# Phi one tile later and in one VectorE operation, small loads, one activation table and a reordered second phase, in a linear-attention and routed-MLP kernel

## The chip, the cores and the metric

The kernel runs on one core of one Trainium2 chip. The metric is the device time of one execution in microseconds (us); lower is better. A profile is one execution recorded by the hardware profiler; its span (first to last instruction) is about 1.7 us shorter than the time of the same execution (before: 192.7 and 194.37). Engines are TensorE (PE in the profile, PEld is its weight load), VectorE (DVE), ScalarE (ACT), GpSimd (POOL) and SyncE (SP), which here only starts DMA transfers. Each engine takes its instructions in program order, so an instruction that waits holds up everything behind it on that engine. (The period shown below has an example: VectorE idles 2.03 us in front of an add that waits for GpSimd, although the statistics behind it need only x.)

## The reference, cut to what matters

One sequence of 2048 tokens with 640 channels, in bf16. The input is layer-normalised; the normed `xn` feeds a linear attention with 32 heads (A) and a block that sends the 8 highest-scoring tokens through a gated MLP (B).

```python
xn = layernorm(x)
# A: linear attention
q, k, v = split(xn @ wqkv)                       # 32 heads of 20
phi = lambda t: where(t > 0, t + 1, exp(t)) + 1e-6
kv  = einsum("bhsd,bhse->bhde", phi(k), v);  z = phi(k).sum(tokens)
A   = ((phi(q) @ kv) / (phi(q) . z + 1e-6)) @ wo
# B: the 8 tokens with the largest r = xn @ w_r
g = silu(x_sel @ w_gate); u = x_sel @ w_up; y = ((g * u) @ w_down) * sigmoid(r_sel)
B = xn + scatter(y)
return x + A + B
```

Since `phi` equals `min(exp(t), 1) + relu(t)`, up to the tiny constant, the kernel needs an Exp and a Relu (ScalarE), a min and an add.

## The kernel before

The kernel never forms v for all tokens. For each of 16 tiles of 128 tokens it computes `k`, then `pk = phi(k)`, and accumulates `G = xn^T pk` in PSUM. A second phase turns G into a small matrix M (through wv and wo), computes q in 20 blocks (4 groups of 512 tokens by 5 groups of channels), divides by the denominators and multiplies by M. The routed MLP runs between those blocks. Helpers that matter:

```python
def ln_stats(t):            # VectorE: mean, variance
    dve.bn_stats(...); dve.bn_stats(...); dve.bn_aggr(out=mv[:], ...)
def ln_mid(t):              # GpSimd: nm = -mean, t2 = var + eps, s = t2 ** 0.5 ; ScalarE: c = x - mean
    pool.tensor_scalar(out=nm[:], ...); act.activation(c[:], XX[:, t, 1, :], AF.Identity, bias=nm[:])
    pool.tensor_scalar(out=t2[:], ...); pool.tensor_tensor(out=s[:], ..., op=ALU.pow)
def ln_xn(t):               # VectorE: xn = c / s   (called "the scale" below)
    dve.reciprocal(sr[:], s[:]); dve.tensor_scalar(out=XX[:, t, 0, :], in0=c[:], scalar1=sr[:], op0=ALU.mult)
def tr_dma(t): ...          # SyncE: DMA transpose of xn into xnT
def K(t): ...               # TensorE: k of the tile, into PSUM banks 6 and 7
def PHa(t): ...             # ScalarE: ek = Exp(k), rk = Relu(k), in halves
def PHm(t):                 # GpSimd
    pool.tensor_scalar(out=ek[:], in0=ek[:], scalar1=1.0, op0=ALU.min)
def PHb(t):                 # VectorE
    dve.tensor_tensor(out=pk[:, t, :], in0=ek[:], in1=rk[:], op=ALU.add)
def xpx(t):                 # GpSimd: x + xn, added to the output at the end
    pool.tensor_tensor(out=XX[:, t, 1, :], in0=XX[:, t, 1, :], in1=XX[:, t, 0, :], op=ALU.add)

for t in range(T):
    K(t); PHa(t)
    if t + 2 < T: ln_xn(t + 2); tr_dma(t + 2)      # (tile 2: transposed on TensorE)
    PHm(t); PHb(t)
    if t + 3 < T: ln_stats(t + 3); ln_mid(t + 3)
    if t >= 1: G(t - 1)
    if t in extras: extras[t]()                    # constants, then copies of wq, on GpSimd
    ...                                            # whole-matrix loads at t = 4, 6, 8, 11
```

The second phase is written by hand as a list of calls. `q_pe` is five matmuls, an Exp and a Relu; `q_fin` is phi's end on VectorE (already one operation here); `den`, `bcast`, `norm` make and apply reciprocals of the denominators, `exp(-ln(den))`; `out_pair` computes two output tiles.

```python
q_pe(0, 0, 0); keysT(); route1(); q_pe(0, 1, 1); q_fin(0, 0); ...
bcast(1, (0, 1, 2, 3)); out_mm(1, 4); ... out_pair(2, 6, 4)      # outputs of group 0 ...
q_pe(3, 0, 1); q_pe(3, 1, 2); ...                                # ... before the q blocks of group 3
out_pair(4, 6, 4); q_fin(3, 4); bcast(2, ...); ...; out_pair(14, 0, 2)
```

## Time and profile before

| | before |
|---|---|
| time, median of the runs beside the changed kernel | 195.64 us (195.08 to 196.32, 4 runs) |
| span of the profiled run | 192.7 us |
| mean granted TensorE clock | 0.953 |
| busy share TensorE / VectorE / ScalarE / GpSimd | 65 / 48 / 43 / 44 % |
| tile loop: first K matmul to first q matmul | 9.65 to 100.62 us |
| second phase: first q matmul to the end | 92.1 us |

First the head of the profile page (busy us, share of the span, number of instructions):

```profile
span 192.7 us, 2691 instructions
PE 124.5 (65%) x950; PEld 68.0 (35%) x961; DVE 92.4 (48%) x204; ACT 83.3 (43%) x176; POOL 84.0 (44%) x123
```

No engine is full. So look at one period of the loop. The next lines are VectorE's timeline (start, duration, engine, source line, operation, output<-inputs, shapes; in brackets the idle time before it and what ended it). L209 is PHb, L130 to L132 the statistics, L156 and L157 the reciprocal and the scale.

```profile
51.92 0.49 DVE L209 TENSOR_TENSOR pk<-ek,rk 128x640 bf16<-128x640 bf16 x1 [2.14 <-POOL ek L205]
...
53.25 0.21 DVE L132 BATCH_NORM_AGGREGATE mv<-stats 128x2 bf16<-128x12 f32 x1
54.74 0.16 DVE L156 RECIPROCAL sr<-s 128x1 f32<-128x1 bf16 x1 [1.28 <-POOL s L150]
55.01 0.51 DVE L157 TENSOR_SCALAR XX<-c,sr 128x640 bf16<-128x640 bf16 x1
57.55 0.49 DVE L209 TENSOR_TENSOR pk<-ek,rk 128x640 bf16<-128x640 bf16 x1 [2.03 <-POOL ek L205]
```

From one PHb to the next is 57.55 - 51.92 = 5.63 us, of which VectorE idles 1.28 for GpSimd's power and 2.03 for GpSimd's min. The window view of that period shows how much work each engine had in it (busy us of each engine, then the granted clock, DMA share and GB/s):

```profile
51.92:57.55 5.63, 2.96 (x18) 1.67 (x19) 2.17 (x7) 2.19 (x6) 3.71 (x6) 1.00 0.92 321
```

TensorE had 2.96 us of work in 5.63. Of the page's groups of instructions, these three name the min itself and the two largest idle times in front of a group (the last column), both waits on GpSimd:

```profile
L205 POOL TENSOR_SCALAR ek<-ek 128x640 bf16<-128x640 bf16 x16 | 29.1, 1823 | 10.4 <-ACT ek L198 9.6
L145 ACT ACTIVATE c<-XX,nm 128x640 bf16<-128x640 bf16 x15 | 12.4, 828 | 47.9 <-POOL nm L144 47.9
L209 DVE TENSOR_TENSOR pk<-ek,rk 128x640 bf16<-128x640 bf16 x16 | 8.4, 527 | 36.9 <-POOL ek L205 36.9
```

In the second phase ScalarE loads a table each time it changes between Exp and Ln:

```profile
110.95 0.21 ACT L514 ACTIVATE ge<-r 1x8 f32<-1x8 f32 x1
111.18 1.28 ACT L515 ACT_TABLE_LOAD   x1
112.47 0.21 ACT L515 ACTIVATE gl<-ge 1x8 f32<-1x8 f32 x1
112.70 1.28 ACT L516 ACT_TABLE_LOAD   x1
114.00 0.21 ACT L516 ACTIVATE g<-gl 1x8 bf16<-1x8 f32 x1
```

There are 14 loads of 1.28 us in all, 12 of them in the second phase. VectorE's later work waits on this chain, and TensorE on VectorE. The window view of the second phase, from the end of the last G matmuls to the last output matmul, gives TensorE 68.5 us of work in 89.2, so 20.7 us of gaps:

```profile
99.30:188.50 89.20, 68.52 (x587) 36.89 (x589) 52.97 (x94) 44.29 (x74) 27.13 (x24) 0.92 0.15 49
```

### The profile page before, as it was taken

Reading aid. Unit: us, or ns where it says so; the run is one execution under the profiler, and the core shown is the slowest. Engines: PE = TensorE matmul, PEld = TensorE weight load, DVE = VectorE, ACT = ScalarE, POOL = GpSimd, SP = SyncE. Lnnn points to the kernel's source line nnn. Section 1 sums busy time; section 2 is a strip of 40 time slices with the busy share of each in tenths; the row PEclk is TensorE's granted clock in tenths of the full one; section 3 lists DMA queues with packets and bytes.
Section 4 is the critical chain, followed back from the end, with each engine's and each line's share of the span. In section 5 each row is a group of like instructions: output and inputs, shape, how many; then the busy total and the mean of one; then the engine's idle time right before and its main releaser. Section 6 shows DMA issues by size and latency. Waiting matters only on the chain. (4 is left out here: it accounts for less than half of the span.)

```text
span 192.7 us, 2691 instructions
## 1 busy us (share of the span) xinstructions
PE 124.5 (65%) x950; PEld 68.0 (35%) x961; DVE 92.4 (48%) x204; ACT 83.3 (43%) x176; POOL 84.0 (44%) x123
## 2 busy tenths in 40 slices
PE   7374447635456446545889959729398669858890
PEld 2142223313223223322556524303144435535460
DVE  2724421445323443432266634895283842963933
ACT  3374314430444432247336599733990049332000
POOL 1534668666576666656420027999950000000000
PEclk9999997999999999999999996996969999978999
DMA  5991121083392871351009200000000110120222
GB/s 170 288 373 54 34 60 37 9 173 60 46 385 57 259 210 34 80 158 34 0 4 312 96 14 2 0 0 0 3 2 0 68 71 0 68 71 0 102 88 84
DMA packets 19622, 16.89 MB, mean 88 GB/s; under 512 B 10001, under 2 KB 18329, under 8 KB 19609
## 3 DMA queue, kind: packets, MB, share of 16 engines
q1 hardware_dynamic: 18281, 15.91, 28.0%
q10 hardware_dynamic: 1328, 0.82, 1.4%
q8 instruction: 7, 0.11, 0.3%
q14 instruction: 6, 0.05, 0.1%
HBM read 11.80 MB, written 2.62 MB: 75 GB/s over the span
## 5 line engine op out<-in xcount | busy, mean ns | idle before, releaser
L214 PE MATMUL PS<-pk,XX 128*128 128x512 bf16 x74 | 23.7, 395 | 20.4 <-DVE pk L209 20.4
L183 PE MATMUL PS<-wk,xnT 128*128 128x320 bf16 (+1 forms) x160 | 25.0, 300 | 18.3 <-ACT rk L199 16.6
L205 POOL TENSOR_SCALAR ek<-ek 128x640 bf16<-128x640 bf16 x16 | 29.1, 1823 | 10.4 <-ACT ek L198 9.6
L145 ACT ACTIVATE c<-XX,nm 128x640 bf16<-128x640 bf16 x15 | 12.4, 828 | 47.9 <-POOL nm L144 47.9
L421 PE MATMUL PS<-xnT,wqp 128*128 128x512 bf16 x95 | 26.3, 410 | 3.2 <-DVE pqT L481 2.3
L621 PE MATMUL PS<-Mb,pqT 128*128 128x320 bf16 x160 | 25.2, 312 | 3.4 <-DVE o L635 2.5
L209 DVE TENSOR_TENSOR pk<-ek,rk 128x640 bf16<-128x640 bf16 x16 | 8.4, 527 | 36.9 <-POOL ek L205 36.9
L175 POOL TENSOR_TENSOR XX<-XX 128x640 bf16<-128x640 bf16 x16 | 25.4, 1620 | 0.0
L183 PEld LDWEIGHTS <-xnT 128*128 128x128 bf16 x160 | 15.5, 97 | 28.0 <-issue 20.3
L433 DVE SCALAR_TENSOR_TENSOR pqT<-qe,qr 128x512 bf16<-128x512 bf16 x20 | 19.5, 978 | 11.7 <-ACT qr L428 11.7
L427 ACT ACTIVATE qe<-PS 128x512 bf16<-128x512 f32 x20 | 11.9, 595 | 23.4 <-PE PS L421 21.0
L621 PEld LDWEIGHTS <-pqT 128*128 128x128 bf16 x160 | 15.9, 101 | 12.0 <-issue 4.2
L635 DVE TENSOR_TENSOR o<-PS,XX 128x640 bf16<-128x640 f32 x16 | 12.4, 818 | 11.3 <-issue 9.1
L198 ACT ACTIVATE ek<-PS 128x320 bf16<-128x320 f32 x32 | 13.7, 430 | 3.3 <-PE PS L183 3.3
L421 PEld LDWEIGHTS <-wqp 128*128 128x128 bf16 x100 | 9.6, 103 | 14.1 <-issue 6.1
L219 PEld LDWEIGHTS <-XX 128*128 128x128 bf16 x64 | 6.4, 100 | 23.2 <-issue 23.2
L219 PE MATMUL PS<-pk,XX 128*128 128x128 bf16 x64 | 14.4, 224 | 0.3
L199 ACT ACTIVATE rk<-PS 128x320 bf16<-128x320 f32 x32 | 14.0, 437 | 0.0
L144 POOL TENSOR_SCALAR nm<-mv 128x1 f32<-128x1 bf16 x15 | 3.5, 232 | 23.2 <-DVE mv L132 21.4
L428 ACT ACTIVATE qr<-PS 128x512 bf16<-128x512 f32 x20 | 11.9, 595 | 0.0
L214 PEld LDWEIGHTS <-XX 128*128 128x128 bf16 x80 | 8.0, 100 | 9.1 <-issue 1.4
L156 DVE RECIPROCAL sr<-s 128x1 f32<-128x1 bf16 x16 | 2.5, 157 | 16.7 <-POOL s L150 16.7
(136 smaller groups left out, 162.1 us busy)
## 6 DMA issues: line engine op xcount, KB each, us to landing
out_dram<-o SPq DMA_DIRECT2D x16, 160.0 KB, 1.8
wg<-in_B_w_gate_dram SPq DMA_DIRECT2D x1, 1920.0 KB
wu<-in_B_w_up_dram SPq DMA_DIRECT2D x1, 1920.0 KB, 9.4
wd<-in_B_w_down_dram SPq DMA_DIRECT2D x1, 1920.0 KB, 7.9
XX<-in_A_x_dram SPq DMA_DIRECT2D x1, 1280.0 KB, 9.7
wq<-in_A_wqkv_dram SPq DMA_DIRECT2D x1, 800.0 KB
wv<-in_A_wqkv_dram SPq DMA_DIRECT2D x1, 800.0 KB
wo<-in_A_wo_dram SPq DMA_DIRECT2D x1, 750.0 KB
```

The costliest lines, as they stand in the source:

```text
L145: act.activation(c[:], XX[:, t, 1, :], AF.Identity, bias=nm[:])
L175: (eng or pool).tensor_tensor(out=XX[:, t, 1, :], in0=XX[:, t, 1, :], in1=XX[:, t, 0, :], op=ALU.add)
L183: pe.matmul(PS[:, 6 + h, 0:w], lhsT=xnT[:, kc, t * P : (t + 1) * P], rhs=wk[:, kc, h * HW : h * HW + w], start=(kc == 0), stop=(kc == KC - 1),
L198: act.activation(ek[:, sl], PS[:, 6 + h, 0:HW], AF.Exp)
L199: act.activation(rk[:, sl], PS[:, 6 + h, 0:HW], AF.Relu)
L205: pool.tensor_scalar(out=ek[:], in0=ek[:], scalar1=1.0, scalar2=None, op0=ALU.min)
L214: pe.matmul(PS[:, a, :], lhsT=lhsT, rhs=pk[:, t, 0:512], start=(t == 0), stop=(t == T - 1),)
L219: pe.matmul(PS[:, 5, a * P : (a + 1) * P], lhsT=lhsT, rhs=pk[:, t, 512:D], start=(t == 0 and a == 0), stop=(t == T - 1), skip_group_check= ...
L421: pe.matmul(PS[:, bank, :], lhsT=wqp[:, kc, m, :], rhs=xnT[:, kc, tb * TBLK : (tb + 1) * TBLK], start=(kc == 0), stop=(kc == KC - 1),)
L433: dve.scalar_tensor_tensor(out=pqT[:, m, tb * TBLK : (tb + 1) * TBLK], in0=e[:], scalar=1.0, in1=r[:], op0=ALU.min, op1=ALU.add,)
L621: pe.matmul(PS[:, b + h, 0:HW], lhsT=pqT[:, kc, t * P : (t + 1) * P], rhs=Mb[:, kc, h * HW : (h + 1) * HW], start=(kc == 0), stop=False)
L635: dve.tensor_tensor(out=o[:].rearrange("p (h c) -> p h c", h=2), in0=PS[:, b : b + 2, 0:HW], in1=XX[:, t, 1, :].rearrange("p (h c) -> p h ...
```

## The change

The intent: keep every engine's queue from waiting on another engine's last result. Its parts, as core of a long diff:

```diff
+    act.preload_act_table_set("natural_log_exp_and_others")     # has Exp and Ln; the warm-up Ln goes
...
-    def PHm(t):
-        pool.tensor_scalar(out=ek[:], in0=ek[:], scalar1=1.0, scalar2=None, op0=ALU.min)
     def PHb(t):
-        dve.tensor_tensor(out=pk[:, t, :], in0=ek[:], in1=rk[:], op=ALU.add)
+        dve.scalar_tensor_tensor(out=pk[:, t, :], in0=ek[:], scalar=1.0, in1=rk[:], op0=ALU.min, op1=ALU.add)
...
     for t in range(T):
-        K(t); PHa(t)
+        K(t)                                  # (tile 0 is split in halves around tile 1's transpose)
+        if t >= 1: PHb(t - 1)                 # phi one tile later
         if t + 2 < T: ln_xn(t + 2); tr_dma(t + 2)
-        PHm(t); PHb(t)
         if t + 3 < T: ln_stats(t + 3)
+        if t in dve_extra: perm_q(dve_extra[t])   # copies of wq: from GpSimd to VectorE
+        PHa(t)
         if t + 3 < T: ln_mid(t + 3)
         if t >= 1: G(t - 1)
+        if 7 <= t: xpx(t)                     # nine of the sixteen x + xn move into the loop
+        loads(t)                              # 300 to 480 KB pieces instead of whole matrices
```

The constants shift by a tile, the 14 warming matmuls become 10, and G's copies out of PSUM are cut by bank. The second phase is reordered: all 20 q blocks with everything that hangs on them first, then the 16 outputs in one run. For groups 2 and 3 half of the `norm` products take their factor through ScalarE.

```diff
-    bcast(1, (0, 1, 2, 3)); out_mm(1, 4); ... out_pair(2, 6, 4); ...
-    q_pe(3, 0, 1); q_pe(3, 1, 2); ...
+    q_pe(3, 0, 0); ...; q_pe(3, 4, 0); q_fin(3, 3); den(2, 4)
+    out_one(0, 2); q_fin(3, 4); bcast(2, (4, 5, 6, 7)); ...; out_one(7, 0); ...
+    out_pair(8, 2, 0); out_pair(10, 4, 6); out_pair(12, 2, 0); out_pair(14, 4, 6)
```

## The prediction

> **What bounds the kernel now.** The span is 192.7 us, and no engine is full: the page's busy table has TensorE at 65%, the others at 43 to 48%. The timeline splits it into a tile loop (first K matmul at 9.65, last G matmul near 98.5) and a second phase (98.5 to 192.7).
>
> - Loop: most of the 16 tiles repeat every 5.62 us. The by-window table gives, for one such tile, TensorE 3.0, VectorE 2.1, ScalarE 2.2, GpSimd 2.8 to 3.7 busy. The period is therefore one chain through in-order queues, read from the timeline: Exp, GpSimd min (1.82), VectorE add (0.49), statistics of a later tile (1.1), GpSimd mean and power (1.3), reciprocal and scale (0.6), back to Exp. In the wait view pk waits 36.9 us for the min and c waits 47.9 us for nm.
> - Second phase: TensorE's work is about 63 us (20 q blocks at 1.08, 16 outputs at 1.56, the rest some 16). About 20 us are gaps and 6 us half-speed clock. The gaps follow table loads (1.28 us each; 2.4 us before den(0), 3.1 before the h transposes, 1.9 near the last den) and VectorE q_fin held up by xpx.
>
> **What the change does.**
> 1. The min leaves GpSimd; min and add become one VectorE operation. Its 512-column twin takes 0.67 undisturbed, so about 0.83. PHb comes a tile later, so it no longer sits between Exp and the statistics.
> 2. What remains is a norm loop: statistics 1.1, mean and power 1.2 to 1.3, reciprocal and scale 0.6, so 3.0 to 3.1 us; TensorE needs about 2.9.
> 3. New cost: xpx (1.62) enters the loop from tile 7. The Trainium skill ("SBUF — State Buffer", section "SBUF: two separate sides") says VectorE and GpSimd share a port pair under an exclusive lock. This trace agrees: a 0.39 us scale took 1.78 under the iota, two q_fins 3.68 under xpx. xpx starts just when the scale wants to run, adding about 1.2; PHb lies on nm, adding about 0.5. I estimate 3.6 us per tile up to tile 9, 4.6 after.
> 4. Of 14 table loads, 13 go (16.7 us of ScalarE). The skill ("ScalarE: Activation LUTs", "Table sets: the hidden batching unit") has exp and ln in one set; the trace shows a load at each alternation. On the path: 1.3 at the start, 6 to 8 in the second phase.
> 5. Small loads stay behind the transposes they might delay. About 7.5 MB over 55 us is 140 GB/s; the DMA slices reach 385. Little cost.
> 6. Putting all q first removes bank and VectorE waits: another 5 to 8 us. Seven xpx still collide with q_fin.
>
> **Sum.** Prologue: 1 to 3 us gained. The loop's end moves from 98.5 to about 70 (scale of tile 2 at 10.5, tile 9 at 36 to 38, tile 15 at 63 to 66, then 6 to 8 to the last G). Second phase: 63 of work, about 9 of gaps, 2 of cold clock, 4 of tail, about 77 instead of 94. Span about 146; the timed figure lies 2 to 3 us above a profiled span. I predict 148 us, 137 to 160. Faster by over 2%: 0.98; within 2%: 0.015; slower: 0.005.
>
> **What would show it.** Scale operations 3 to 4 us apart early and 4 to 5 late, some stretched past 1.5 us under xpx; one table load; no GpSimd min; gaps on TensorE in the second phase below 12 us in all.
>
> **What would make it wrong.** Transposes landing later than the 2.6 us seen, because load pieces now interleave: K would wait. The port lock costing nearly nothing (loop at 3.1, total near 137) or stacking with the permutation copies (loop above 5, total near 160). Denser TensorE work at a lower granted clock than 0.95. VectorE becoming the limit in the q section.

## The result, and the profile after

| | before | after |
|---|---|---|
| time, median | 195.64 us (4 runs) | 144.02 us (142.63 to 144.19, 4 runs) |
| span of the profiled run | 192.7 | 142.3 |
| mean granted TensorE clock | 0.953 | 0.975 |
| first q matmul | 100.62 | 71.99 |
| from there to the end | 92.1 | 70.3 |
| TensorE busy share | 65 % | 83 % |

The ratio is 0.7345, 95% interval 0.7289 to 0.74. A ratio is the mean time of one kernel's fast runs over that of the other's of the same rounds, so not quite the ratio of the medians quoted.

The head of the page after:

```profile
span 142.3 us, 2672 instructions
PE 118.6 (83%) x952; PEld 65.5 (46%) x952; DVE 99.7 (70%) x216; ACT 68.8 (48%) x166; POOL 58.6 (41%) x99
```

VectorE in an early period (L164, L165: reciprocal and scale; L220: phi; L138 to L141: statistics):

```profile
16.99 0.16 DVE L164 RECIPROCAL sr<-s 128x1 f32<-128x1 bf16 x1 [1.07 <-POOL s L158]
17.26 0.39 DVE L165 TENSOR_SCALAR XX<-c,sr 128x640 bf16<-128x640 bf16 x1
...
18.48 0.21 DVE L141 BATCH_NORM_AGGREGATE mv<-stats 128x2 bf16<-128x12 f32 x1
18.61 0.77 DVE L220 SCALAR_TENSOR_TENSOR pk<-ek,rk 128x640 bf16<-128x640 bf16 x1
20.45 0.17 DVE L164 RECIPROCAL sr<-s 128x1 f32<-128x1 bf16 x1 [1.08 <-POOL s L158]
```

The period is 20.45 - 16.99 = 3.46 us, and VectorE's only idle time in it is 1.08 us for the power of the tile whose statistics it has just finished. GpSimd's line for the same moment shows its mean stretched from 0.24 to 0.61 us while phi runs:

```profile
18.85 0.61 POOL L152 TENSOR_SCALAR nm<-mv 128x1 f32<-128x1 bf16 x1 [1.90 <-DVE mv L141]
```

A late period, with xpx in the loop, on VectorE:

```profile
48.02 1.24 DVE L165 TENSOR_SCALAR XX<-c,sr 128x640 bf16<-128x640 bf16 x1
...
50.62 0.82 DVE L220 SCALAR_TENSOR_TENSOR pk<-ek,rk 128x640 bf16<-128x640 bf16 x1
52.20 0.16 DVE L164 RECIPROCAL sr<-s 128x1 f32<-128x1 bf16 x1 [0.76 <-POOL s L158]
52.47 1.24 DVE L165 TENSOR_SCALAR XX<-c,sr 128x640 bf16<-128x640 bf16 x1
```

and on GpSimd:

```profile
47.68 1.40 POOL L184 TENSOR_TENSOR XX<-XX 128x640 bf16<-128x640 bf16 x1
...
50.70 0.81 POOL L157 TENSOR_SCALAR t<-mv 128x1 bf16<-128x1 bf16 x1
```

The scale begins at 48.02, 0.34 after xpx, and ends at 48.02 + 1.24 = 49.26, 0.18 after xpx's end at 47.68 + 1.40 = 49.08. Its duration undisturbed is 0.39. The other way round, t2 on GpSimd takes 0.81 instead of 0.22 while phi has begun before it (at 50.62, to 51.44). The period here is 52.47 - 48.02 = 4.45 us.

The Trainium skill ("SBUF — State Buffer", section "SBUF: two separate sides") describes this as an exclusive lock on a port pair that VectorE and GpSimd share, held by whichever started first for its whole instruction. The pairs of lines above agree in both directions.

The timeline shows one table load instead of 14:

```profile
0.80 1.28 ACT L95 ACT_TABLE_LOAD   x1 [0.80 <-PEq L822]
```

In the second phase, the window view from the last G matmuls to the last output matmul (columns as above, in three stretches) shows how little TensorE still waits:

```profile
71.50:89.80 18.30, 18.30 (x142) 10.14 (x140) 14.13 (x43) 14.58 (x34) 5.11 (x10) 1.00 0.36 112
89.80:109.80 20.00, 17.48 (x177) 7.66 (x176) 18.02 (x27) 12.56 (x24) 9.81 (x6) 0.91 0.01 1
109.80:138.00 28.20, 28.02 (x273) 16.97 (x272) 17.28 (x27) 4.48 (x10) 0.00 (x0) 1.00 0.23 83
```

TensorE is busy 63.8 of 66.5 us: 2.7 us of gaps. Its one long gap is this. den(1) is written into PSUM bank 3, where the product h, the second operation of `gu_ev`, still has to read u, so den(1) waits for h; h sits on VectorE behind two q_fin that take 2.65 us together under xpx (1.28 where no xpx runs):

```profile
99.54 0.46 PE L486 MATMUL PS<-pqT,zm 128*32 128x128 bf16 x20 [2.04 <-DVE hh L643]
```

### The profile page after: what moved, and what is told of

Its sections match the earlier page's. It is cut to its first block, busy times and chain, and to the rows that moved or that the text cites. A ratio compares the mean times of both kernels' runs of the same rounds, so it can differ in the third digit from the quotient of the medians.

```text
span 142.3 us, 2672 instructions
## 1 busy us (share of the span) xinstructions
PE 118.6 (83%) x952; PEld 65.5 (46%) x952; DVE 99.7 (70%) x216; ACT 68.8 (48%) x166; POOL 58.6 (41%) x99
## 4 chain that ended last, share of the span: by engine, by line
PE 44%; DVE 27%; POOL 17%; issue 5%; DMA 2%; ACT 1%; DVEq 1%; POOLq 0%
PE PS L672 16%; PE PS L464 11%; DVE XX L165 8%; POOL s L158 6%; POOL t L157 5%; POOL nm L152 4%; DVE stats L140 4%; DVE stats L138 4%; DVE pqT L476 3%; PE PS L225 2%; DVE mv L141 2%; DMA XX<-in_A_x_dram 2%; PE PS L680 2%; DVE sr L164 2%; DVE pk L220 1%
## 5 line engine op out<-in xcount | busy, mean ns | idle before, releaser
L225 PE MATMUL PS<-pk,XX 128*128 128x512 bf16 x80 | 23.4, 378 | 10.2 <-DVE pk L220 10.2
L195 PE MATMUL PS<-wk,xnT 128*128 128x320 bf16 (+1 forms) x160 | 25.9, 310 | 3.4 <-DMA xnT<-XX 1.7
L464 PE MATMUL PS<-xnT,wqp 128*128 128x512 bf16 x100 | 24.9, 385 | 0.0
L672 PE MATMUL PS<-Mb,pqT 128*128 128x320 bf16 x160 | 24.1, 300 | 0.0
L672 PEld LDWEIGHTS <-pqT 128*128 128x128 bf16 x160 | 14.7, 98 | 7.2 <-issue 0.4
L476 DVE SCALAR_TENSOR_TENSOR pqT<-qe,qr 128x512 bf16<-128x512 bf16 x20 | 17.2, 870 | 1.1 <-ACT qr L471 1.1
L220 DVE SCALAR_TENSOR_TENSOR pk<-ek,rk 128x640 bf16<-128x640 bf16 x16 | 15.1, 946 | 2.0 <-ACT rk L214 2.0
L464 PEld LDWEIGHTS <-wqp 128*128 128x128 bf16 x100 | 9.1, 99 | 9.8 <-issue 1.5
L152 POOL TENSOR_SCALAR nm<-mv 128x1 f32<-128x1 bf16 x15 | 6.1, 403 | 18.0 <-DVE mv L141 17.8
L165 DVE TENSOR_SCALAR XX<-c,sr 128x640 bf16<-128x640 bf16 x16 | 11.4, 712 | 1.6
L164 DVE RECIPROCAL sr<-s 128x1 f32<-128x1 bf16 x16 | 2.6, 163 | 12.9 <-POOL s L158 12.8
```

Of the source, the lines that this page charges most:

```text
L195: pe.matmul(PS[:, 6 + h, 0:w], lhsT=xnT[:, kc, t * P : (t + 1) * P], rhs=wk[:, kc, h * HW : h * HW + w], start=(kc == 0), stop=(kc == KC - 1),
L220: dve.scalar_tensor_tensor(out=pk[:, t, :], in0=ek[:], scalar=1.0, in1=rk[:], op0=ALU.min, op1=ALU.add)
L225: pe.matmul(PS[:, a, :], lhsT=lhsT, rhs=pk[:, t, 0:512], start=(t == 0), stop=(t == T - 1),)
L464: pe.matmul(PS[:, bank, :], lhsT=wqp[:, kc, m, :], rhs=xnT[:, kc, tb * TBLK : (tb + 1) * TBLK], start=(kc == 0), stop=(kc == KC - 1),)
L476: dve.scalar_tensor_tensor(out=pqT[:, m, tb * TBLK : (tb + 1) * TBLK], in0=e, scalar=1.0, in1=r, op0=ALU.min, op1=ALU.add,)
L672: pe.matmul(PS[:, b + h, 0:HW], lhsT=pqT[:, kc, t * P : (t + 1) * P], rhs=Mb[:, kc, h * HW : (h + 1) * HW], start=(first and kc == 0), sto ...
```

## The experiments

There were eleven runs of ten kernels, in three sets on three chips. "After" is 144.02 us, and the kernel before, run beside each set, had medians of 194.8 to 196.1. Times are medians of all executions, slow ones included: one of four in the runs of the lag without the fusion and of the whole-matrix loads, two of six in the repeat of the statistics ahead, one of six in the run of xpx held back. Without them these four are 169.84, 144.17, 134.76 and 133.44 us. Ratios are to the kernel before unless said otherwise, use fast executions alone, and are the safer figures between sets. In the second set (no xpx, xpx behind the loop, whole-matrix loads, statistics ahead) three of seven executions of the kernel before were slow, and the record's verdict for these four runs is "unclear"; their ratios are given as recorded.

### Table set alone

The kernel before, plus the preload, minus the warm-up Ln:

```diff
+    act.preload_act_table_set("natural_log_exp_and_others")
-    act.activation(wrm[:], one11[:], AF.Ln)
```

> The kernel before, with only one thing changed: the table set that has both exp and ln is loaded once at the start and the warm-up Ln is gone. Theory (13 table loads of 1.28 us go, of which 7 to 9 us lie on the path: 1.3 before the first Exp and 6 to 8 in the second phase): 187 to 189 us. The loop keeps its 5.62 us per tile. Rival (ScalarE is idle over half of the time, so the loads hide in its idle time): within 2 us of 196.

Measured: 185.33 us against 195.41, ratio 0.9465 (0.9389 to 0.9541). So 10.1 us come from 13 loads of 1.28 us, 16.7 in all. The loads lay on the path, and more of them than expected. The first q matmul moved only from 100.62 to 100.26, so nearly all of it is in the second phase. The gap of 2.4 us before den(0) and that of 3.1 before the h transposes are gone from TensorE's timeline.

### Fused phi alone

The kernel before, with PHm gone and PHb as one operation, in its old place:

```diff
-        PHm(t)
         PHb(t)              # now scalar_tensor_tensor(min, add)
```

> The kernel before, with only the min folded into the VectorE add; still done in the same tile, in front of the statistics. Theory (one chain, Exp, clamp and add, statistics, mean, centring, next Exp): the chain loses 1.82 of min and a hop and gains about 0.35, so 4.4 us per regular tile instead of 5.62 and 176 to 179 us in all. Rival (only taking phi out from between Exp and the statistics helps, as the loop is bound by that order): the period stays above 5.2 and the time above 190.

Measured: 176.96 us, ratio 0.9043 (0.8994 to 0.9092). The scales are 4.46 or 4.47 us apart in most tiles, instead of 5.62, and the first q matmul is at 82.52 instead of 100.62. Two of them:

```profile
49.08 0.51 DVE L157 TENSOR_SCALAR XX<-c,sr 128x640 bf16<-128x640 bf16 x1
53.55 0.51 DVE L157 TENSOR_SCALAR XX<-c,sr 128x640 bf16<-128x640 bf16 x1
```

The chain theory holds to 0.1 us in the period; the rival (period above 5.2) falls.

### The lag without the fusion

The changed kernel, with the min put back on GpSimd behind the power of the same iteration:

```diff
+        if t > 0: PHm(t)    # GpSimd min, after ln_mid(t + 3)
-        dve.scalar_tensor_tensor(out=pk[:, t, :], ..., op0=ALU.min, op1=ALU.add)
+        dve.tensor_tensor(out=pk[:, t, :], in0=ek[:], in1=rk[:], op=ALU.add)
```

> The changed kernel, with the min put back on GpSimd (after mean and power of that tile) and the add as it was; everything else, the lag of phi by a tile too, is kept. Theory (the fused clamp is what makes the lag pay): mean and power 1.25, min 1.82, add 0.49, scale 0.6, statistics 1.1 stay in one chain, so 5.2 us per tile up to tile 9 and about 6 where xpx shares GpSimd; total 166 to 174. Rival (the lag alone hides the min, since phi has a whole tile of slack): period at most 4, total under 150.

Measured: 170.27 us, ratio to before 0.8745 (0.8682 to 0.8809). Most periods are 5.30 to 5.32 early and 6.48 or 6.49 from the scale of tile 10 on, where xpx shares GpSimd. VectorE's add waits for the min, and the scale stands behind the add:

```profile
42.11 0.39 DVE L165 TENSOR_SCALAR XX<-c,sr 128x640 bf16<-128x640 bf16 x1
46.75 0.49 DVE L220 TENSOR_TENSOR pk<-ek,rk 128x640 bf16<-128x640 bf16 x1 [2.81 <-POOL ek L224]
47.42 0.39 DVE L165 TENSOR_SCALAR XX<-c,sr 128x640 bf16<-128x640 bf16 x1
```

The first q matmul is at 98.40, hardly before the 100.62 of the kernel before, which has no xpx in its loop. So with the min at this place on GpSimd, moving phi a tile later gains 0.3 us per early tile. GpSimd itself idles 1.7 us before the mean at 43.63; whether the min would cost less at an earlier place in its queue was not run. The four corners are:

| period of early tiles, us | phi in its own tile | phi a tile later |
|---|---|---|
| min on GpSimd | 5.62 (before) | 5.31 |
| min and add fused | 4.47 | 3.46 to 3.61 (after) |

This is not a clean cross: the two columns come from kernels that also differ in their loads, tables, copies of wq and second phase. The rows differ in the phi operations alone.

### The old second phase behind the new loop

Everything of the changed kernel up to the last G, then the calls and helpers of before; of the xpx only tiles 0 to 6 remain there.

```diff
-    (second phase of the changed kernel)
+    (second phase of the kernel before; q temporaries in the ek and rk buffers; xpx of tiles 7 to 15 left in the loop)
```

> The changed kernel's loop, small loads and single table, but the second phase in the order of before (outputs between q blocks, G evacuation as before, reciprocals from PSUM on VectorE only); xpx of tiles 0 to 6 alone remain in it. Theory (the order of the q blocks and outputs is worth 5 to 8 us beyond the tables): 150 to 155 us. Rival (with the tables gone and half of the xpx moved out, the old order is as good): under 147 us.

Measured: 158.58 us, ratio 0.8121 (0.8085 to 0.8158). The first q matmul is at 72.67, within 0.7 us of the changed kernel's, so nearly all of the 158.58 - 144.02 = 14.6 us lies in the second phase. That is twice what was predicted for the order. (It is the order together with its helpers: G's copies by bank and the factors through ScalarE went back too, and were not tried alone.) From the last G matmuls to the last output matmul TensorE is busy 66.4 of 81.1 us:

```profile
71.50:152.60 81.10, 66.40 (x585) 36.40 (x588) 51.02 (x94) 28.99 (x62) 14.18 (x15) 0.92 0.16 54
```

So it has 14.7 us of gaps against 2.7 in the changed kernel, 12 of the 14.6 us; the other 2.6 are longer busy time. Two of the gaps are these, at the broadcasts before norm4 and in front of the q blocks of group 3:

```profile
95.43 0.26 PE L503 MATMUL PS<-rden,hmp 32*128 32x128 bf16 x1 [2.99 <-DVE pqT L512]
118.59 0.58 PE L456 MATMUL PS<-xnT,wqp 128*128 128x512 bf16 x1 [2.25 <-DVE pqT L516]
```

and with them stretches at a lower granted clock: two output tiles at 136.62 took 3.98 us where they usually take 2.92 (mean clock 0.76 from 135 to 142). The mean granted clock of that profile is 0.943, against 0.975.

### No xpx in the loop

The changed kernel without xpx for tiles 7 to 15. The result is wrong: those rows lack a term.

```diff
-        if 7 <= t: xpx(t)
```

> The changed kernel without the xpx of tiles 7 to 15 (those output rows are wrong on purpose: they lack the normed term). Theory (port lock: the scale of tiles 10 to 15 waits for xpx, 1.24 instead of 0.39, and the last two phi for 3.9 instead of 1.6): scales 3.5 to 3.6 apart to the end instead of 4.3 to 4.45; the loop ends 6 to 8 us earlier, total 136 to 138. Rival (the late tiles are slow because load pieces sit in front of the transposes): scale intervals stay at 4.3 or more, total within 2 us of 144.

Measured: 138.68 us. Apart from one period of 4.13 among the constants, the scales from tile 2 on stay 3.45 to 3.61 us apart to the last tile, and every one takes 0.39 to 0.47 us; the first q matmul is at 66.72, 5.3 us earlier. The long late periods of the changed kernel are xpx, not loads. Nor is it xpx's time in GpSimd's own queue: in those periods GpSimd idles 1.31 us for the statistics, which stand behind the stretched scale. As for the sizes: the gain of 5.3 us is a little less than the 6 to 8 expected, and the total just above the 136 to 138 expected. Some 4.3 of the 5.3 us lie between the scales of tiles 9 and 15, and about 0.8 behind them.

### xpx behind the loop

The same, with the nine xpx placed after the seven of the second phase. The result is right.

```diff
-    for t in range(0, 7): xpx(t)
+    for t in range(0, T): xpx(t)
```

> The changed kernel, xpx of tiles 7 to 15 moved out of the loop, behind the first seven (right result). Theory: the loop gains the same 6 to 8 us as without them, but nine more xpx of 1.65 now run under the q blocks, whose VectorE ends share the port; there the stretched operations cost back 3 to 6 us, so 138 to 143. Rival (second phase is bound by TensorE and does not feel them): 136 to 138, as without xpx.

Measured: 142.2 us (141.12 to 142.77), ratio 0.7319 against the changed kernel's 0.7345. Of 5.3 us gained in the loop, 142.2 - 138.68 = 3.5 are paid back under the q blocks. The rival (second phase does not feel them) falls. Whether 142.2 is faster than 144.02 is not settled: the intervals of the ratios overlap.

### Whole-matrix loads

The changed kernel with the loads of before.

```diff
-        loads(t)            # pieces
+        loads(t)            # x 8 to 15 and wq at the start; wo, wg, wu, wv whole at t = 4, 6, 8, 11
```

> The changed kernel with the loads as before: x tiles 8 to 15 and wq at once at the start, wo, wg, wu, wv as whole matrices at tiles 4, 6, 8, 11. Theory (the loop has about 1 us of slack at the transposes, and a big load holds the queue for 5 us): K waits up to 3 us behind each of wg and wu, and the first tiles 1 to 2 us behind the early loads; 146 to 151 us. Rival (the loads are off the path in either form): within 1 us of 144.

Measured: 144.29 us (143.72 to 145.96), ratio 0.7424 (0.7359 to 0.7489). The rival holds for the time as far as the runs resolve it: the interval overlaps that of the changed kernel, 0.7289 to 0.74, so a cost of 1 or 2 us is not excluded. But half of the theory is in the trace: the longest transpose landed 6.7 us after its issue instead of 3.6, and K waited 9.2 us for transposes in three places instead of 1.7 (total, times, longest; the changed kernel second):

```profile
PE PS L197 <- DMA xnT<-XX: 9.2, 3, 3.8
PE PS L195 <- DMA xnT<-XX: 1.7, 3, 0.7
```

The scales drop behind (periods of 5.13 and 4.99) and one catches up with 3.17; the first q matmul is at 72.95 instead of 71.99. The reading is that K had slack, because the norm loop, not TensorE, set the pace; the last experiment tests it.

### Statistics one tile further ahead

The idle 1.07 us of VectorE in the changed loop is the wait for the power of the tile whose statistics have just ended. If iteration t takes the statistics of tile t + 4, that result is needed an iteration later.

```diff
-        if t + 3 < T: ln_stats(t + 3)
+        if t == 0: ln_stats(3)
+        if t + 4 < T: ln_stats(t + 4)
-        if t + 3 < T: ln_mid(t + 3)
+        if t == 0: ln_mid(3)
+        if t + 4 < T: ln_mid(t + 4)          # mv, nm, t2, s, c: one more buffer each
```

> The changed kernel with the statistics and centring one tile further ahead (tile t+4 in iteration t), so that VectorE does not wait for GpSimd's power of the tile whose statistics it has just finished; one more buffer each. Theory (the norm loop statistics, mean, power, scale sets 3.46 to 3.6 us per tile): early tiles drop to TensorE's 3.0, tiles under xpx to 3.7 to 4.0, bound by the shared port; 137 to 140 us. Rival (period is set by K waiting for transposes and by TensorE itself): no change, 143 to 145.

Measured: 134.95 us (134.39 to 135.5), correct, ratio to before 0.6952 (0.6892 to 0.7013), an interval below that of the changed kernel. It beats the expectation. The first q matmul is at 62.28 instead of 71.99. The window view of the loop, from tile 0's K to the matmuls that follow G(14), first of the changed kernel and then of this one, shows the same matmuls in 9.7 us less:

```profile
9.40:68.20 58.80, 45.54 (x294) 26.27 (x292) 41.95 (x95) 32.52 (x92) 39.00 (x69) 0.98 0.67 166
```

```profile
9.40:58.50 49.10, 43.81 (x287) 26.09 (x291) 37.82 (x95) 32.86 (x92) 39.56 (x69) 0.97 0.82 198
```

TensorE is busy 43.8 of 49.1 us (89%, from 45.5 of 58.8), and its G waits for phi only 0.9 us in all, where it waited 10.2 in the changed kernel:

```profile
PE PS L225 <- DVE pk L220: 10.2, 12, 1.6
PE PS L225 <- DVE pk L220: 0.9, 2, 0.5
```

(A few matmul records are missing from such traces, so the counts differ.) Early, from tile 2 to tile 9, the scales are 3.2 us apart on average, unevenly (2.22 to 3.94), where 3.0 was expected. Under xpx they are 3.26 to 3.31 us apart, not the 3.7 to 4.0 expected; there GpSimd is the limit, with no idle time in its round, of which some 0.7 us is stretching under VectorE's operations (a mean of 0.72 and a t2 of 0.40 us instead of 0.24 and 0.22). Its next mean starts at 44.02, right behind an xpx that ends at 42.55 + 1.39 = 43.94, and its round from mean to mean is 44.02 - 40.73 = 3.29 us:

```profile
40.73 0.72 POOL L152 TENSOR_SCALAR nm<-mv 128x1 f32<-128x1 bf16 x1
...
42.55 1.39 POOL L184 TENSOR_TENSOR XX<-XX 128x640 bf16<-128x640 bf16 x1
44.02 0.72 POOL L152 TENSOR_SCALAR nm<-mv 128x1 f32<-128x1 bf16 x1
```

The rival (transposes or TensorE set 3.46 already) falls.

A second set, on another chip, repeats it: 135.56 us, ratio 0.6895 (0.686 to 0.693).

> The kernel with the statistics one tile further ahead again, for comparison on one chip with the next two. 134.4 to 135.5 us, as the first time.

### xpx held back to where GpSimd is idle

In the kernel with statistics ahead, the last xpx pile up at the end of the loop, where they stretch the last phis to 2.01 and 1.59 us; GpSimd then idles 15 us. A one-element copy that reads the last pk holds seven of them back.

```diff
-        if 7 <= t: xpx(t)
+        if 7 <= t < 11: xpx(t)
...
+    pool.tensor_copy(gate[:], pk[0:1, T - 1, 0:1])
+    for t in (11, 12, 13, 14, 15, 0, 1): xpx(t)
...
-    for t in range(0, 7): xpx(t)
+    for t in range(2, 7): xpx(t)          # the load of wd, which takes pk's place, moves behind the copy
```

> Statistics one tile further ahead, and the xpx of tiles 11 to 15, 0 and 1 held back by a one-element GpSimd copy that waits for the last phi, so that they fill the time in which GpSimd was idle (58 to 73 us in that trace) instead of stretching the last phis (2.0 and 1.6 us instead of 0.8) and the q section. Theory (the lock is what is left to win at these two places): the loop ends 2 to 3 us earlier, the 2 us wait for the h product shrinks; 131 to 133 us. Rival (the same xpx only stretch other VectorE operations at the start of the second phase): 134 to 136.

Measured: 133.6 us (132.59 to 134.82), correct; ratio 0.681 (0.6779 to 0.684) against 0.6895 (0.686 to 0.693) on the same chip and in the same rounds. It is the fastest kernel, by 1.2%, less than expected (131 to 133). Both profiles of this pair fell in a slow execution (single-core runs more than 1.5% above the fastest), so they are compared only with each other. The last phis take 0.82 to 0.83 us again, the first q matmul comes 1.1 us earlier (64.41 against 65.51) and the wait for the h product shrinks from 2.03 to 0.83 us; against that, three q_fin of the first group now take 1.67 and, two together, 3.14 us. The spans differ by 1.6 us.

### Whole-matrix loads where there is no slack

The kernel with statistics ahead, with the loads of before.

> Statistics one tile further ahead, but loads as whole matrices, as before the change. In the changed kernel big loads made K wait up to 3.8 us for single transposes and yet cost nothing. Theory (those waits were absorbed by slack, since the norm loop was slower than TensorE; with that slack used up they show): 138 to 143 us. Rival (the form of the loads does not matter at all): within 1 us of the kernel with statistics ahead, 134 to 136.

Measured: 142.05 us, ratio 0.7244 (0.7217 to 0.7272), against 0.6895 for the same kernel with small loads on the same chip. The same loads that cost nothing that the runs resolve in the changed kernel cost 6.5 us here. The cost is in the loop: the first q matmul is at 70.36, against 62.28 in the first run of the kernel with statistics ahead, and from there to the end both take 70.2 to 70.4 us. K waits 10.2 us for transposes in four places, the longest of them:

```profile
36.24 1.54 PE L197 MATMUL PS<-wk,xnT 128*128 128x320 bf16 x10 [3.69 <-DMA xnT<-XX]
```

So the small loads of the change had no effect on its own time that these runs resolve, but they are needed once the loop has no slack left.

## Why the prediction was right, point by point

The prediction of 148 us (137 to 160) was right: 144.02 measured. Point by point:

- "The period is therefore one chain through in-order queues." Right that it is a chain, and that the min, the add and the statistics are links. Wrong in its last links: it runs on through "power" and "reciprocal and scale" (1.3 + 0.6), while the timeline goes from the mean to the centring on ScalarE (0.83) and to the next Exp. The experiment with the fused phi used these corrected links: taking the min out alone gave 4.47 us where they said 4.4.
- "What remains is a norm loop". Right, and shown by the experiment that moves the statistics a tile further ahead: the same matmuls were done in 49.1 us instead of 58.8.
- "I estimate 3.6 us per tile up to tile 9, 4.6 after." Measured 3.46 to 3.61 (one period of 4.13 among the constants), then 4.31 to 4.45. The lock on the port pair was taken from the skill and from two lines of the trace before; without xpx the late periods are as short as the early ones. The stretched scales take 1.23 or 1.24 us; that some would pass 1.5 us, as forecast, did not show. That GpSimd's mean lies under phi is in the trace (0.61 instead of 0.24 us); what it costs was not tested by itself, as the wait could not be taken away alone.
- "scale of tile 2 at 10.5, tile 9 at 36 to 38, tile 15 at 63 to 66, then 6 to 8 to the last G." Measured 10.31, 35.52, 61.09, and about 10.4 to the last G matmul (71.5). The last term was too small. The phis of tiles 13 and 14 stand under piled-up xpx and took 3.94 us for the two, and G(13), with K(15) behind it, waited 1.36 us. But the xpx explain only about 0.8 us: without any xpx in the loop the same stretch takes 9.6 us (56.63 to 66.19). The rest lies in that stretch itself, with K(14), G(13), K(15), G(14), the corner and z matmuls (1.9 us) and G(15) one behind the other.
- "On the path: 1.3 at the start, 6 to 8 in the second phase" for the tables. The table alone gave 10.1 us, nearly all in the second phase: undersized there, and the 1.3 at the start shrank to 0.4 by the loop's end (100.62 to 100.26).
- "Putting all q first ... another 5 to 8 us." This term was mis-sized by about half: the old order with its helpers costs 14.6 us. The prediction allowed "about 9 of gaps, 2 of cold clock" on TensorE to remain after the change; of the 20.7 us of gaps before, 66.5 - 63.8 = 2.7 us are left. The work itself, "about 63 us", was right. I had expected the seven xpx left in the second phase to hold TensorE up; in the new order most of their delay hides behind other TensorE work, except for one wait of 2.04 us.
- "Small loads ... Little cost." Right for the time. They were also of no use in this kernel, which the prediction did not say.

So the total is 4 us below the central value because the second phase gained more (142.3 - 71.5 = 70.8 us from the last G matmul to the end, against "about 77"), partly offset, by luck, by the longer end of the loop. Terms 4 and 6 were both too small for the second phase, and they overlap: its gain, from 93 to 70.8 us, is less than 10.1 + 14.6. (The last G matmul of the kernel before starts at 99.24, not at the 98.5 of the prediction.)

How the 51.6 us divide cannot be given as a sum of independent parts. The tables are worth 10 us by themselves and the order with its helpers 14.6 us at the end. The fusion is worth 18.5 us alone and 26 us if it is taken out of the changed kernel: the lag gains 0.3 us per early tile without it and 0.9 to 1.0 with it.

## What to carry to other kernels

When no engine is full, lay one period of the loop out as a chain and count the waits of the in-order queues: a result needed right after it was ordered costs its whole latency, and asking for it one iteration earlier (here one more buffer of each kind) can bring the loop close to what its busiest engine needs. Ask which engine a moved operation will meet: in these traces xpx on GpSimd stretched VectorE's scale (0.39 to 1.24 us) and q_fin, which reads two tiles of SBUF (0.67 to 1.83), but not the norm products, which read PSUM (four took 2.47 us under xpx and 2.48 without). So such work belongs beside operations of the last kind, or where VectorE idles. And test the parts of a change again after the bottleneck has moved: small loads were worth nothing that the runs resolve at 144 us, and 6.5 us at 135.

## What the Trainium skill lacked or had wrong

- "ScalarE: Activation LUTs", section "What ACT_TABLE_LOAD costs": the load itself is as stated (1283 ns in the page, 1283 ns in every load here), but the drain of about 1380 ns that the page adds for each switch does not show. From the end of `ge` (110.95 + 0.21 = 111.16) to the start of `gl` (112.47) is 1.31 us, not 2.66.
- "SBUF — State Buffer", section "SBUF: two separate sides": the lock is as described. What the page lacks is a figure for short GpSimd operations, which pay too: [128,1] operations of 0.22 to 0.24 us took 0.61 to 0.81 under a VectorE operation of 0.8 us with two SBUF inputs.
- No page that was read gives a duration for VectorE's min-and-add in one operation: on 128x640 bf16 it took 0.77 to 0.83 us undisturbed, the add alone 0.49, the min on GpSimd 1.82.
- "DMA: Bandwidth & Descriptors": its sections on transposes and latency give a transfer rate, but no landing time for a 128x640 transpose from SBUF to SBUF behind other transfers of the same queue. Here it landed 2.5 us after issue at best. With loads of 300 to 480 KB around it, it took at most 3.6 us in the changed kernel and 5.2 with the statistics ahead (fast run), with whole matrices of up to 1920 KB at most 6.7 and 8.4.
